# Fifty-two steps in seven products instead of twenty-two, with the scan's work cut into pieces between them

## The chip, the core and the metric

The kernel runs on one core of a Trainium2 chip. A core has TensorE (matrix products, PE in the profile, its weight loads PEld), VectorE (DVE), ScalarE (ACT), GpSimd (POOL) and SyncE (SP, which here only issues DMAs). Each engine takes its own instructions strictly in the order in which the kernel issues them, and waits on semaphores for data of the others. TensorE writes into PSUM, eight banks of 128 x 512 float32. The metric is the device time of one execution in microseconds (us).

## The reference

Two blocks follow each other. The first is a state-space scan over 4 sequences of 8 heads and 768 positions, in chunks; the second is a feed-forward layer over all 3072 tokens with the gate h * cos(h):

```python
M = CB * L                                   # L = exp(cum_i - cum_j), causal
y_intra = np.einsum('bhij,bhjd->bhid', M, xc)
y_inter = np.einsum('bhin,bhnd->bhid', Cc, state) * decay_to_i[..., None]
state = decay_full * state + np.sum(Bx, axis=2)
...
h = x @ w_in          # x: the scan's y, 3072 x 256;  w_in: 256 x 2048
g = h * np.cos(h)
out = g @ w_out       # w_out: 2048 x 256
```

All of it is in float32.

## The kernel before, in words

The 768 positions are NC = 6 chunks of 128, each of two units of 64. The feed-forward part is a loop of NC * NF = 96 steps n; with NF = 16, c = n // 16 is the chunk and f = n mod 16. In chunks after the first, steps f = 0 to 7 belong to the first unit (u = 0) and 8 to 15 to the second; a step works on 256 columns of h, turned (hp, 128 x 512, one PSUM bank), for one unit of all four sequences.

One step is a chain over the engines: TensorE makes hp (`first`, L660), ScalarE rounds hp / 2 pi to an integer k (`wind_k`, L667), VectorE subtracts it (`wind_w`, tile w, L673), ScalarE takes the sine (`gate`, L682), VectorE multiplies by hp (`gated`, tile gT, L687), and TensorE multiplies by w_out into o (`second`), LAG = 3 steps later. PSUM holds two banks for hp (tag "h"), two for o, and two pairs of banks (tag "scan") that the scan uses.

From chunk 1 on, o is made by a Strassen-like scheme with seven products (`seven`, L831); GpSimd makes the differences of gT (`differ`, L712 to L715). At the end of a unit `end7` copies o's two banks on ScalarE (L849, L852), and the copies are summed into the output (`rest`, L864) on VectorE or GpSimd; `finished` holds the second copy back to the start of the next step where that one is in `sevens`.

In 22 of the 96 steps hp too is made by seven products (`begin7`, `period7`, L760): steps 42 to 44, 58 to 60, 74 to 76 and 81 to 93. A step of seven issues on TensorE: products 1, 5 and 7 of its hp; two products of o; the last pair (3 and 4) of the previous step's hp; the next two products of o; the late pair (6 and 2); three more of o. Between the first three and the late pair, ScalarE copies what the first three left (L764, L765); after the late pair VectorE adds the copies (L768, L770) before the last pair may come. Its k, w, sine and gT run a step later. A third hp bank is taken from a pair where three such steps follow each other. The scheme needs differences of y (`differ_y`, tile m, L742) and of w_in (`differ_in`, L731).

The scan of chunk e = c + 1 runs beside the steps of chunk c, at places set by the table `steps`: decays (`decays0`, a scan on VectorE, L375, of 128 x 512), the reach (`reaches`, L574: eight scans of 64 elements), transposes of the blocks of B and C (`turn_blocks`, L582), masked copies of C on ScalarE and a product with the reach (`turn2`, L591 and L593), the products g of C and B (`inner2`, L603), their weighing on VectorE (`weights`, L465), the state (`add_state`, four operations, L498), the products with the state (`open2`, L617, and the sums of the new state, L477), the rest of y (`finish2`, L629), and its copies (L636, L489). `open2` stands at f = 13, `finish2` at f = 15.

All loads go through SyncE's queue in the order of issue: the `blocks` of a chunk (L147, L150), `along` (the decays spread over partitions, L188), `arow` (L165), B, C and x, and the outputs.

Of the kernel before, what the change touches and what calls it, by code (L numbers as in the profile page):

```python
# [25 lines left out]
def kernel(  # L26
# [51 lines left out]
    ones = const.tile([P, P], FP32, name="ones")  # L78
    V.memset(ones, 1.0)
# [98 lines left out]
    def load_along(c, seqs=range(NB)):  # L178

        if c >= NC:  # L180
            return
        if c not in along:
            along[c] = rows.tile([P, NB, P], FP32, tag="along", bufs=2, name="along")
        for b in seqs:
            s = b // 2
            for q in range(4 if s else 1):
                rs, hs = (group(q, s), slice(2 * q, 2 * q + 2)) if s else (slice(0, P), slice(0, H))
                nc.sync.dma_start(  # L188
                    out=along[c][rs, b], in_=a_all[b, hs, c * P:(c + 1) * P].unsqueeze(1)
                    .to_broadcast([hs.stop - hs.start, N, P]))  # L190
# [7 lines left out]
    lead, along1, reach1 = (ms[2][:, i * NB * (W + 1):(i + 1) * NB * (W + 1)]  # L198
                            .rearrange("p (b i) -> p b i", b=NB) for i in range(3))
# [155 lines left out]
    reach, part, yT, after = {}, {}, {}, {}  # L355
# [12 lines left out]
    def decays0(k, p, i=0, n=1):  # L368
# [5 lines left out]
        rows_ = spread.pop((k, p, i)) if k < 2 else arows[k][:, p]  # L374
# [118 lines left out]
    def add_state(k):  # L493

        for s in range(2):
            for p in range(2):
                i = k % 2 * W + W - 1
                V.scalar_tensor_tensor(out=after[k][:, s, p], in0=after[k - 1][:, s, p],  # L498
                                       scalar=reach[k // 2, s][:, p, i:i + 1],
                                       in1=after[k][:, s, p], op0=ALU.mult, op1=ALU.add)  # L500
# [66 lines left out]
    def reaches(c, b):  # L567

        s, p = divmod(b, 2)
        if p == 0:  # L570
            reach[c, s] = scan.tile([P, 2, P], FP32, tag="reach", name="reach")
        for k in range(2):
            i = slice(k * W, (k + 1) * W)
            V.tensor_tensor_scan(out=reach[c, s][:, p, i], data0=along[c][:, b, i],  # L574
                                 data1=ones[:, 0:W], initial=1.0, op0=ALU.mult, op1=ALU.mult)
# [3 lines left out]
    def turn_blocks(c, s):  # L579
        turned[c, s] = t = scan.tile([P, 2, 2, P], FP32, tag="turned", bufs=2, name="turned")  # L580
        for k in range(2):
            V.transpose(out=t[:, k].rearrange("p s (t m) -> p s m t", m=4),  # L582
                        in_=blocks[c, s][:, k].rearrange("p h s (m n) -> p (s m) h n", m=4))
        del blocks[c, s]

    def turn2(c, s):

        tp = turned.pop((c, s))
        cT = scan.tile([P, 2, 2, P], FP32, tag="cT2", bufs=2, name="cT2")
        for t in range(2):  # L590
            ACT.activation(cT[:, :, t], tp[:, 1], AF.Copy, scale=slot[:, t:t + 1])  # L591
        rT = scan.tile([P, 2, P], FP32, tag="rT", name="rT")
        V.tensor_tensor(out=rT, in0=tp[:, 1], in1=reach[c, s], op=ALU.mult)  # L593
        part[c, s] = (tp[:, 0], cT, rT)

    def inner2(c):

        g = [pair("g") for _ in range(2)]
        for k, p, s, q in ((k, p, s, q) for k in range(2) for p in range(2) for s in range(2)
                           for q in range(4)):  # L600
            bT, cT, _ = part[c, s]
# [9 lines left out]
    def open2(c):  # L611

        ys[c] = y = [pair("y") for _ in range(2)]
        for k, p, s, q in ((k, p, s, q) for k in range(2) for p in range(2) for s in range(2)
# [3 lines left out]
                      rhs=part[c, s][2][r, p, k * W:(k + 1) * W], start=(k == p == 0), stop=False,  # L618
# [350 lines left out]
    def rest_of_loads():  # L969
# [21 lines left out]
        for k in (4, 5):  # L991
            for s in range(2):
# [4 lines left out]
    steps = {c: dict(reach=(5, 6), turn=(6, 7), inner=8, weigh=(9, 10), state=(-NF, 12),  # L997
                     decays=(8, 11, 13, 14), along=(12, 13)) if c == 2 else
             dict(reach=(1, 2), turn=(3, 4), inner=5, weigh=(6, 7), state=(0, 5),
                  decays=(8, 9, 14, 15), along=(6, 7)) for c in range(2, NC)}  # L1000
# [12 lines left out]
    def decays2(k, p):  # L1013
        decays0(k, p)
        if p == 1:
# [7 lines left out]
    AHEAD = 4  # L1023
# [3 lines left out]
    runs = [*(range(NF * c + 10, NF * c + 13) for c in range(2, NC - 1)),  # L1027
            range(NC * NF - 15, NC * NF - 2)]
    sevens = {n: r for r in runs for n in r}
    at_ = {}  # L1030

    def bank_of(n):

        i = n - sevens.get(n, sevens.get(n - 1))[0]
        if i == 0:
            at_["hp"] = pair("hp")[:, 0]
        return at_["hp"] if i % 3 == 1 else bank([P, TB], "hp", "h")
# [6 lines left out]
    def period7(n):  # L1044
# [17 lines left out]
        return last_  # L1062
# [55 lines left out]
    for n in range(AHEAD, NC * NF + LAG):  # L1118
        c, f = divmod(n, NF)
        if n < NC * NF:  # L1120

            if c > 0 and f in (loads_of := (6, 7, 8, 9) if c == 1 else (0, 1, 2, 3)):
                load(c + 2, loads_of.index(f))
# [10 lines left out]
            second_ = lambda n=n: second(n - LAG)  # L1134
            if n in sevens:
                second_ = period7(n)
            elif n - 1 in sevens:
                first(n, rest7[n - 1][2], to_=bank_of(n))
                gates(n - 1)
            else:  # L1140
                first(n)
            closing = f == NF - 1 and 1 <= c < NC - 1
            take_y = finish2(c + 1) if closing else None
            if n not in sevens:
                wind_k(n)
                wind_w(n)
# [8 lines left out]
            if n not in sevens:  # L1155
                gate(n)
# [5 lines left out]
            if joins:  # L1162
# [4 lines left out]
            behind += [lambda c=c, b=2 * s + p: reaches(c, b) for c, s in chunks_at(n, "reach")  # L1167
                       for p in range(2)]
# [100 lines left out]
```

## Time and profile before

| | |
|---|---|
| three runs | 366.31, 367.38, 367.40 us; median 367.38 |
| profiled execution | 366.6 us, span 364.7 us, granted clock of TensorE 0.999 |
| TensorE | 356.8 us busy, 98% of the span |
| VectorE, ScalarE, GpSimd | 259.0, 191.6, 234.1 us busy |
| hp plain (L660) | 592 matmuls of 128x256, 141.7 us |
| hp in seven (L760) | 308 matmuls of 128x128 |
| DMA | 26.42 MB, 72 GB/s on average |

A float32 product shows as two matmul records. The records of matmuls overlap, so the distance between starts, not the mean length of a record, is what a product costs. In the lines of a timeline the columns are start, duration, engine, line, operation, output and inputs, shapes, count of merged instructions, and in brackets the idle time before and what ended it.

### The profile page before, as it was taken

The numbers are of one execution on the slowest core, as the hardware profiler recorded it, in microseconds if no ns is written. First come the engines' busy times: TensorE is split into PE (matmuls) and PEld (weight loads), VectorE is DVE, ScalarE is ACT, GpSimd is POOL, SyncE is SP. The second block draws the span as 40 slices with busy tenths as digits, with TensorE's granted clock in tenths as the row PEclk, the third lists the DMA queues.
The fourth block names the chain that finished last, engine by engine and source line by source line (L and its number), as shares of the span: only waits on it lengthen the run. The fifth ranks groups of instructions, "written<-read, shape, count | busy, mean of one in ns | idle before, by whom it ended". The sixth has DMA issues, their size and how long they took to land.

```text
span 364.7 us, 10134 instructions
## 1 busy us (share of the span) xinstructions
PE 356.8 (98%) x4034; PEld 326.0 (89%) x4034; DVE 259.0 (71%) x448; ACT 191.6 (53%) x368; POOL 234.1 (64%) x375
## 2 busy tenths in 40 slices
PE   8997999999999999999999999999999999999995
PEld 5686888888999999999999999989999999999995
DVE  7789998587867867976665887556786455566663
ACT  4597766445445254635554544545553644566651
POOL 6567757579856873467587467487656384375572
PEclk9999999999999999999999999999999999999999
DMA  7996956691665528214007621001010001001002
GB/s 140 260 373 137 224 132 81 112 119 51 128 102 75 92 60 129 44 44 86 8 4 111 74 71 34 3 3 40 0 31 0 2 2 31 2 3 31 2 0 59
DMA packets 97327, 26.42 MB, mean 72 GB/s; under 512 B 87328, under 2 KB 93184, under 8 KB 97280
## 3 DMA queue, kind: packets, MB, share of 16 engines
q1 hardware_dynamic: 96032, 25.38, 34.7%
q8 instruction: 32, 0.52, 0.6%
q10 hardware_dynamic: 1248, 0.39, 0.5%
q14 instruction: 15, 0.12, 0.1%
HBM read 22.36 MB, written 3.34 MB: 70 GB/s over the span
## 4 chain that ended last, share of the span: by engine, by line
PE 95%; DVE 2%; ACT 1%; issue 1%; ACTq 0%; DVEq 0%
PE hp L660 35%; PE o L831 34%; PE hp L760 9%; PE o L790 7%; PE y L629 2%; PE g L603 1%; PE y L477 1%; PE y L617 1%; PE g L456 1%; PE a_ps L364 1%; PE warm L84 1%; PE y L525 1%; PE y L515 1%; PE o L891 0%; DVE mag L261 0%
## 5 line engine op out<-in xcount | busy, mean ns | idle before, releaser
L660 PE MATMUL hp<-yT,w_in 128*128 128x256 f32 x592 | 141.7, 382 | 2.1 <-DVE gT L687 2.1
L660 PEld LDWEIGHTS hp<-yT,w_in 128*128 128x128 f32 x592 | 107.5, 190 | 16.4 <-POOL mag L249 2.5
L673 DVE SCALAR_TENSOR_TENSOR w<-hp,k 128x512 f32<-128x512 f32 x96 | 66.1, 688 | 68.6 <-ACT k L667 68.4
L712 POOL TENSOR_TENSOR gd<-gT 128x256 f32<-128x256 f32 x79 | 60.0, 760 | 82.6 <-DVE gT L687 67.7
L682 ACT ACTIVATE w<-w,quarter 128x512 f32<-128x512 f32 x96 | 69.4, 723 | 66.3 <-DVE w L673 66.0
L667 ACT ACTIVATE k<-hp 128x512 int32<-128x512 f32 x96 | 57.2, 596 | 74.7 <-PE hp L660 68.0
L687 DVE TENSOR_TENSOR gT<-hp,w 128x512 f32<-128x512 f32 x96 | 65.6, 684 | 23.3 <-ACT w L682 17.7
L831 PE MATMUL o<-words,gd 128*128 128x128 f32 x474 | 69.4, 275 | 0.0
L831 PEld LDWEIGHTS o<-words,gd 128*128 128x128 f32 x474 | 61.0, 192 | 0.0
L831 PE MATMUL o<-w_out,gT 128*128 128x128 f32 x316 | 49.7, 276 | 0.3 <-ACT ps L849 0.3
L831 PEld LDWEIGHTS o<-w_out,gT 128*128 128x128 f32 x316 | 46.1, 191 | 3.5 <-ACT ps L849 0.5
L715 POOL TENSOR_TENSOR gd<-gT,gd 128x128 f32<-128x128 f32 x79 | 40.8, 516 | 6.2
L714 POOL TENSOR_TENSOR gd<-gT,gd 128x128 f32<-128x128 f32 x79 | 39.3, 497 | 6.2
L831 PE MATMUL o<-w_out,gd 128*128 128x128 f32 x158 | 30.6, 275 | 0.0
L831 PE MATMUL o<-words,gT 128*128 128x128 f32 x158 | 30.5, 275 | 0.0
L790 PE MATMUL o<-w_out,gT 128*128 128x256 f32 x128 | 30.1, 379 | 0.0
L375 DVE TENSOR_TENSOR_SCAN lam<-arow,unit 128x512 f32<-128x512 f32 x20 | 29.0, 1448 | 0.0
L790 PEld LDWEIGHTS o<-w_out,gT 128*128 128x128 f32 x128 | 24.2, 190 | 3.2
L831 PEld LDWEIGHTS o<-words,gT 128*128 128x128 f32 x158 | 24.0, 192 | 0.0
L831 PEld LDWEIGHTS o<-w_out,gd 128*128 128x128 f32 x158 | 24.0, 192 | 0.0
L760 PE MATMUL hp<-m,wid 128*128 128x128 f32 x132 | 22.3, 278 | 0.0
L760 PEld LDWEIGHTS hp<-m,wid 128*128 128x128 f32 x132 | 18.2, 192 | 0.2
(129 smaller groups left out, 424.0 us busy)
## 6 DMA issues: line engine op xcount, KB each, us to landing
words<-in_moe_w_in_dram SPq DMA_DIRECT2D x8, 512.0 KB
words<-in_moe_w_out_dram SPq DMA_DIRECT2D x8, 512.0 KB
xr<-in_x_dram SPq DMA_DIRECT2D x24, 128.0 KB
arow<-a_cut SPq DMA_DIRECT2D x10, 256.0 KB
arow<-a_cut SPq DMA_DIRECT2D x10, 252.0 KB
out_dram<-sum SPq DMA_DIRECT2D x18, 128.0 KB
bc<-in_B_dram SPq DMA_DIRECT2D x24, 64.0 KB
blocks<-in_B_dram SPq DMA_DIRECT2D x16, 32.0 KB
```

The costliest lines, as they stand in the source:

```text
L375: V.tensor_tensor_scan(out=lams[k][:, p, hs].rearrange(flat), data0=rows_.rearrange(flat), data1=unit0[:, hs].rearrange(flat), initial=0.0 ...
L660: PE.matmul(to_[:, e], lhsT=w_in[:, k, fs], rhs=y[:, k], start=(k == 0), stop=(k == KT - 1), skip_group_check=True)
L667: ACT.activation(k, hp[n], AF.Copy, bias=0.25, scale=INV_2PI)
L673: V.scalar_tensor_tensor(out=w, in0=hp[n], scalar=INV_2PI, in1=k, op0=ALU.mult, op1=ALU.subtract)
L682: ACT.activation(cos, cos, AF.Sin, bias=quarter, scale=TWO_PI)
L687: V.tensor_tensor(out=gT[n], in0=hp.pop(n), in1=cos, op=ALU.mult)
L712: G.tensor_tensor(out=d[:, 0:2], in0=g[:, 1:2].to_broadcast([P, 2, P]), in1=g[:, 3::-3], op=ALU.subtract)
L714: G.tensor_tensor(out=d[:, 2], in0=g[:, 0], in1=d[:, 0], op=ALU.subtract)
L715: G.tensor_tensor(out=d[:, 3], in0=g[:, 2], in1=d[:, 2], op=ALU.subtract)
L760: PE.matmul(at[:, i], lhsT=w[q], rhs=y_[q], start=(q == 1), stop=True, skip_group_check=True)
L790: PE.matmul(o[c, u][:, t], lhsT=g[:, 2 * e + t], rhs=w_out[:, 2 * j + e], start=(j == e == t == 0), stop=(j == NJ - 1 and e == 1), skip_gr ...
L831: PE.matmul(at[q], lhsT=a_[q], rhs=w[q], start=(j == 0 and q in starts), stop=(j == NJ - 1), skip_group_check=True)
```

## The change

Steps in seven products become 52: 33 to 36, 39 to 44, 46 to 52, 55 to 60, 62 to 68, 71 to 76 and 78 to 93. From step 32 on a second main loop runs, in which the scan's work is handed to the steps as a list (`scan_work`), at most one or two small pieces each; `steps` remains for chunk 2 alone.

- The chunk's g and its weighing become one visit at f = 5 (`visit_g`), and the whole of y (`open2`, `finish2`, copies) one visit at f = 13 (`visit_y`); steps 5 and 13 make hp plainly, and so does step 6.
- The reach of two sequences becomes one scan of 260 elements; for it `along` has a leading zero for every run of 64, and its loads are split in two (20 instead of 10 DMAs a chunk). `lead` (a one ahead of 64 zeros) becomes a tile of its own, and the tile of ones goes.
- The state is advanced by two operations over all of it instead of four.
- Half of the decays are done in halves (128 x 256), in steps 7 to 10; the others in the visit of y.
- The differences of the next y for its first unit are made on GpSimd, two at f = 14 and two at f = 15; the output sums from step 32 on are all on GpSimd, one a step.
- In steps 5 to 23 o follows hp by two steps; step 5 makes o of steps 2 and 3, step 24 makes none, and from step 25 the lag is three again.
- The differences of w_in are made at other steps (`in_at`).

The diff, cut:

```diff
-    ones = const.tile([P, P], FP32, name="ones")
-    V.memset(ones, 1.0)
+    lead = const.tile([P, NB, W + 1], FP32, name="lead")
...
-            along[c] = rows.tile([P, NB, P], FP32, tag="along", bufs=2, name="along")
+            along[c] = rows.tile([P, NB, 2, W + 1], FP32, tag="along", bufs=2, name="along")
+            G.memset(along[c][:, :, :, 0:1], 0.0)
...
-                nc.sync.dma_start(
-                    out=along[c][rs, b], in_=a_all[b, hs, c * P:(c + 1) * P].unsqueeze(1)
-                    .to_broadcast([hs.stop - hs.start, N, P]))
+                for k in range(2):
+                    nc.sync.dma_start(
+                        out=along[c][rs, b, k, 1:],
+                        in_=a_all[b, hs, (2 * c + k) * W:(2 * c + k + 1) * W].unsqueeze(1)
+                        .to_broadcast([hs.stop - hs.start, N, W]))
...
     def add_state(k):
-        for s in range(2):
-            for p in range(2):
-                i = k % 2 * W + W - 1
-                V.scalar_tensor_tensor(out=after[k][:, s, p], in0=after[k - 1][:, s, p],
-                                       scalar=reach[k // 2, s][:, p, i:i + 1],
-                                       in1=after[k][:, s, p], op0=ALU.mult, op1=ALU.add)
+        r = reach[k // 2][:, :, :, k % 2, W:].to_broadcast([P, 2, 2, 2 * D])
+        dec = scan.tile([P, 2, 2, 2 * D], FP32, tag="whole", bufs=1, name="whole")
+        V.tensor_tensor(out=dec, in0=after[k - 1], in1=r, op=ALU.mult)
+        V.tensor_tensor(out=after[k], in0=after[k], in1=dec, op=ALU.add)
...
+    def reaches(c, s):
+        V.tensor_tensor_scan(
+            out=reach[c][:, s].rearrange(flat), data0=along[c][:, 2 * s:2 * s + 2].rearrange(flat),
+            data1=lead.rearrange("p b i -> p (b i)"), initial=0.0, op0=ALU.mult, op1=ALU.add)
...
+    in_at = {24: slice(1, 3), 28: slice(3, 5), 32: slice(0, 1), 35: slice(7, 8), 41: slice(5, 7)}
-    runs = [*(range(NF * c + 10, NF * c + 13) for c in range(2, NC - 1)),
-            range(NC * NF - 15, NC * NF - 2)]
+    runs = [r for c in range(2, NC - 1) for r in (
+                range(NF * c + (1 if c == 2 else -2), NF * c + 5), range(NF * c + 7, NF * c + 13))]
+    runs.append(range(NF * (NC - 1) - 2, NC * NF - 2))
...
+        third = n % 3 == 1 if c == NC - 1 else f in (2, 7, 10, 15)
+        return pair("hp")[:, 0] if third else bank([P, TB], "hp", "h")
...
-    def period7(n):
+    def period7(n, extra=()):
...
-        return last_
+        for do in extra:
+            do()
+        last_()
...
+        if n == AHEAD + 1:
             second(n - LAG)
-        elif n > AHEAD:
-            second_()
+        if n > AHEAD and n != LATER:
+            second(n - (LAG if n > LATER else LAG - 1))
...
+    def visit_g(n, e):
+        inner2(e)
+        rest7[n - 1][2]()
+        wind_k(n - 1)
+        second(n - LAG)
+        weights(2 * e, 0)
+        wind_w(n - 1)
+        weights(2 * e, 1)
+        gate(n - 1)
+        gated(n - 1)
+        first(n)
+        for q in range(2):
+            weights(2 * e + 1, q)
+        gates(n)
+    def visit_y(n, e, halves):
+        open2(e)
+        rest7[n - 1][2]()
+        wind_k(n - 1)
+        take_y = finish2(e)
+        second(n - LAG)
+        first(n)
+        for do in halves[:1]:
+            do()
+        wind_w(n - 1)
+        gate(n - 1)
+        for do in halves[1:]:
+            do()
+        gated(n - 1)
+        for k in range(2):
+            take_y(k)
+        gates(n)
...
+    def scan_work(c, f):
+        e, k = c + 1, 2 * c + 4
+        work = {15: [lambda: mask_c(e + 1, 0, 0)], 14: [lambda: add_state(2 * e + 1)],
+                0: [lambda: reaches(e, 0)],
+                1: [lambda: turn_blocks(e, 1, (1,))],
+                2: [lambda: turn_blocks(e, 1, (0,)), lambda: mask_c(e, 1, 0)],
+                3: [lambda: reaches(e, 1), lambda: mask_c(e, 1, 1)],
+                4: [lambda: reach_c(e, 0)],
+                6: [lambda: reach_c(e, 1), lambda: add_state(2 * e)],
+                11: [lambda: turn_blocks(e + 1, 0, (1,))],
+                12: [lambda: turn_blocks(e + 1, 0, (0,))]}
+        work[0].append(lambda: mask_c(e, 0, 1))
...
+        for i in range(4 if e < NC - 1 else 0):
+            work[7 + i] = [lambda i=i: half_decay(k, i // 2, i % 2)]
...
+        if live and f in (14, 15):
+            for i in range(2 * (f - 14), 2 * (f - 14) + 2):
+                differ_y(e, i, G, slice(0, 1))
```

For c = 2 the list differs: the transposes of the first half of chunk 3 come at step 32, and the reach of chunk 3 at steps 35 and 36.

## The prediction

> Times are in us. A step is one n of the main loop, f = n mod 16 its place in a chunk, T the start of its first hp product on TensorE.
>
> **What bounds the kernel now.** I read the busy shares first, then the chain that ended last, then TensorE's timeline, the other engines' timeline in a run of seven-product steps, and SyncE's queue.
>
> ```profile
> span 364.7 us, 10134 instructions
> PE 356.8 (98%) x4034; PEld 326.0 (89%) x4034; DVE 259.0 (71%) x448; ACT 191.6 (53%) x368; POOL 234.1 (64%) x375
> PE 95%; DVE 2%; ACT 1%; issue 1%; ACTq 0%; DVEq 0%
> ```
>
> TensorE is never idle for long: its work is the time. So a saving counts in full only if TensorE goes on without waiting, and every wait that is added counts in full too. The timeline gives the length of both kinds of step:
>
> ```profile
> 197.72 1.89 PE L660 MATMUL hp<-yT,w_in 128*128 128x256 f32 x8
> 201.01 1.89 PE L660 MATMUL hp<-yT,w_in 128*128 128x256 f32 x8
> ...
> 326.86 0.39 PE L760 MATMUL hp<-yT,w_in 128*128 128x128 f32 x2
> 328.87 0.39 PE L760 MATMUL hp<-m,wid 128*128 128x128 f32 x2
> 329.99 0.39 PE L760 MATMUL hp<-yT,w_in 128*128 128x128 f32 x2
> ```
>
> A plain step takes 201.01 - 197.72 = 3.29, a step of seven 329.99 - 326.86 = 3.13. The line at 328.87 is the "late pair" of the seven (products 6 and 2): it is due at T + 2.01, and at T + 1.56 where the step before was plain and left no last pair. It must wait for the two ACT copies of its step. What runs around it:
>
> ```profile
> 326.13 0.69 DVE L673 SCALAR_TENSOR_TENSOR w<-hp,k 128x512 f32<-128x512 f32 x1 [0.88 <-ACT k L667]
> 326.74 0.42 DVE L768 TENSOR_TENSOR hp<-hp,m 128x256 f32<-128x256 f32 x1
> 326.86 0.72 ACT L682 ACTIVATE w<-w,quarter 128x512 f32<-128x512 f32 x1 [0.76 <-DVE w L673]
> 327.19 0.30 DVE L770 TENSOR_TENSOR hp<-hp,m 128x128 f32<-128x128 f32 x1
> 327.68 0.69 DVE L687 TENSOR_TENSOR gT<-hp,w 128x512 f32<-128x512 f32 x1 [0.19 <-ACT w L682]
> 327.73 0.37 ACT L764 COPY m<-hp 128x256 f32<-128x256 f32 x1 [0.16 <-PE hp L760]
> 328.14 0.25 ACT L765 COPY hp<-hp 128x128 f32<-128x128 f32 x1
> 328.51 0.73 POOL L712 TENSOR_TENSOR gd<-gT 128x256 f32<-128x256 f32 x1 [0.64 <-DVE gT L687]
> 328.63 0.60 ACT L667 ACTIVATE k<-hp 128x512 int32<-128x512 f32 x1 [0.24 <-PE hp L760]
> 329.32 0.46 POOL L714 TENSOR_TENSOR gd<-gT,gd 128x128 f32<-128x128 f32 x1
> 329.86 0.46 POOL L715 TENSOR_TENSOR gd<-gT,gd 128x128 f32<-128x128 f32 x1
> ```
>
> With T = 326.86: the sine of the step before ends at T + 0.72, the copies run from T + 0.87 to T + 1.53, k starts at T + 1.77, gT of the step before ends at T + 1.51, POOL's differences of it end at T + 3.46. VectorE is free from T + 1.51 to T + 2.40 (next w): a piece of up to 0.9 fits there. ACT has only 0.15 between sine and copies.
>
> **What the change takes away.** 30 more steps of seven at 3.29 - 3.13 = 0.16 each: 4.7. The starts of the three old middle runs had about 0.1 each: 0.3. This is all of the gain. The pieces on VectorE (half decays, two half transposes, one reach scan; nearest rows 0.62 to 0.75 for half of a 1.21 to 1.45 scan, 0.64, 1.12 for the 128x260 scan) lie in the 0.9 gap; 1.12 overshoots by 0.26, and the sums have 0.4 before the last pair waits for them. I cost them at nothing; without that slack see the third rival. VectorE gains 30 x 0.72 of sums and loses 12 output sums (8.0 + 1.8, now on POOL) and some state work, about 12 net on 259: not a bound over the whole. POOL has room over a chunk too (about 45 of 57), but its order matters below. The removed fill of ones and the moved memsets lie in the first us or beside other work: nothing.
>
> **The lag.** Step 5 now takes o of two steps. In the trace hp of step 6 starts at 34.35 after 2.08 idle, set by gT of step 4, so the extra 1.73 fits into that idle time. The same o is then missing at step 24. There TensorE comes at 104.51 to inner2, which needs the C masks that ACT finishes at 105.34 + 0.91 = 106.25; it started at 106.16 before. So the missing o is only an earlier wait: gain 0, at most 1.6 if the masks came early. In steps 5 to 23 the shorter lag leaves w_out's pieces and gd in time by the rows (closest: step 20, 0.2 late): 0.2, left out.
>
> **SyncE's queue.** load_along goes from 10 issues a chunk to 20. What stands behind them in the queue:
>
> ```profile
> 82.95 5.08 SPq L188 DMA_DIRECT2D along<-a_all  x8
> 99.41 2.19 SPq L150 DMA_DIRECT2D blocks<-in_C_dram  x2
> ...
> 104.64 0.66 DVE L582 STREAM_TRANSPOSE turned<-blocks 128x256 f32<-128x256 f32 x1 [0.96 <-DMA blocks<-in_C_dram]
> ```
>
> SyncE issues back to back from 52 to 145. Eight issues take 5.08, 0.635 each (median 0.583 for 16 KB and for 64 KB alike), so ten more take 6.35 even at half the bytes. About 1.5 of small waits (ob, arow) between 88 and 99 absorb part: the C blocks of chunk 2 come 4.85 later, and their transpose waits for them already today. gT of step 23 and inner2 stand behind it: **+4.85** (bounds 1.6, at half the issue time, and 6.35). The along loads of chunk 3 push the C blocks of chunk 3 again by 6.35, less 0.5: issued to 138.25 + 10.6, plus 3.0 landing (101.60 to 104.64) makes 151.9. Their transpose now stands in step 33, VectorE at 137.33 + 4.85 + 2.9 = 145.1. w, the sums and the sine of 33, and the output copy of step 34 follow; o of step 35, due at 148.8, starts at 154.95: **+6.1**, with the copy of the next paragraph in it (bounds 1.1 and 8).
>
> **Output copies.** Twice a chunk o leaves its banks inside a run of seven, after steps f=2 and f=10. Step 83 of the trace shows the price: the copy starts at 314.41, behind the sine, o waits until 314.92, and the step takes 317.48 - 313.79 = 3.69, that is 0.56 more. At f=10 this is new three times: 1.7. At f=2 a mask (0.45) now stands ahead of the copy on ACT: 1.1 each in chunks 3 and 4: 2.2.
>
> **Visit of y (f=13).** hp of step 13 is the last thing before step 14's seven. k (T + 0.26 to 0.86), w, sine end at T + 2.4, then come the copies on ACT, to T + 3.1; the late pair is due at T + 1.56. Before, a whole o (1.56) lay between. Stall 1.57, and 1.84 where four state scalings (1.18) stand ahead of k: 1.84 + 1.84 + 1.57 = **5.25**.
>
> **Difference of y.** POOL's last two differences of the next y are issued at f=15 behind gd of step 14, which ends at T + 3.46 of step 0; the third (0.46) ends at T + 3.99; the late pair of step 0, due at T + 2.01, reads it. Stall 1.95, at steps 48, 64, 80: **5.85**.
>
> **Visit of g (f=5).** VectorE gets four weights (4 x 0.68) among w and gT of steps 4 to 6, reach_c 0.42 and add_state about 1. By these rows gT of step 4 ends at the moment hp of step 6 wants its bank (0.3), the sine of step 6 ends 1.8 after step 7 began, and step 7's late pair waits 1.0: 1.3 x 3 = **3.9**, the least sure term (0 to 6).
>
> Sum: -4.7 - 0.3 + 4.85 + 6.1 + 1.7 + 2.2 + 5.25 + 5.85 + 3.9 = +24.9. The profiled execution took 366.6 (span 364.7 and 1.9 around it), 0.8 under the median of the three runs, 367.38. 366.6 + 24.9 = **391.5**.
>
> **A rule weighed.** The two DMA waits leave TensorE idle for some 6 each; the longest idle stretch of the trace after the start is 2.08, and the granted clock stayed at full in it, so no row prices a longer one and the sum has 0. The Trainium skill, "TensorE: Matmul & The Clock Gate", section "What's actually happening", says that an idle window of about 3.4 halves the clock until about 3.4 of busy time have passed. By that page an estimate of up to 1.7 comes on top at each gap, and the sum would be 395.
>
> **Rivals.** (1) Faster: the steps of seven follow each other as in the last run of the trace, 13 steps at 3.13 with one stall, and every new wait finds its data. That gives 366.6 - 5.0 = 361.6. For it: the 0.9 gap on VectorE. Against it: the waits after f=13 and f=15 follow from single engines' order and durations. It decides where all stalls together stay under 4.7; the two alone are 11.1. (2) The queue is hidden: SyncE's issues get cheaper with their bytes, or the blocks are there in time. Then 11 of the sum goes, but the f=2 copy of chunk 2 (1.1) is back: 366.6 + 24.9 - 9.85 = 381.7. Against it stands the 0.96 that VectorE waits today. (3) VectorE is the bound: w, sums and gT take 2.1 plus gaps of 0.25, a contended piece 1.0; then ten steps a chunk overrun by about 0.2 each, 6 in all: 397.5. (4) The waits are there but half of them overlap: 366.6 - 5 + 15 = 376.6.
>
> **How the numbers follow.** Forecast 0.56 (386 to 397), hidden queue 0.20 (377 to 386), VectorE 0.07, half of the waits 0.08, faster 0.07, no change 0.02 (within 0.3%, what a measurement of this kernel can tell). The range 372 to 398 leaves out the last two, some of the fourth case and of the third: under 0.2. Slower 0.91.
>
> **What would show it.** TensorE's idle time grows from about 8 to over 30. In the waits: hp late pairs on ACT's copy at steps 7 and 14 of a chunk, on POOL's difference at step 0, o on the output copy; VectorE on the blocks' DMA at steps 23 and 33; L188's count at 80. The forecast is wrong if the late pairs don't wait, or if SyncE's queue has caught up by step 23.

## The result, and the profile after

The changed kernel takes 399.94 us (median of four executions, 398.41 to 401.46) against 367.31 for the kernel before (four executions, 366.31 to 367.40): a ratio of 1.0895, 95% interval [1.0847, 1.0943]. Ratios here and below go by the executions within 1.5% of the fastest of the same kernel, which leaves out four of the ten of c4_split_visit (370.63 to 372.92) and one of the kernel before beside it. The prediction was 391.5 with a range of 372 to 398; slower was right, the size was not. The profiled execution took 398.41, 31.8 more than that of before.

The head of the page and the chain that ended last, after:

```profile
span 396.6 us, 10628 instructions
PE 360.0 (91%) x4214; PEld 330.7 (83%) x4214; DVE 266.6 (67%) x457; ACT 208.3 (53%) x428; POOL 254.1 (64%) x419
PE 54%; SPq 15%; POOL 8%; ACT 7%; DVE 7%; issue 4%; DMA 4%; DVEq 0%; POOLq 0%; ACTq 0%
```

TensorE's share of the chain fell from 95% to 54%. What came in is SyncE's queue (15%) and, in small parts, every other engine. TensorE's busy time rose by 3.2, though it has less to do; that is a first sign of a slower clock in places. What TensorE waits for, after (total, times, longest):

```profile
PE hp L768 <- POOL m L750: 5.7, 4, 1.7
PE g L611 <- ACT cT L589: 5.7, 2, 5.0
PE o L839 <- ACT ps L857: 4.4, 7, 1.8
PE hp L768 <- DVE hp L778: 3.8, 2, 3.0
PE hp L768 <- ACT hp L773: 3.6, 3, 1.2
PE hp L668 <- DVE gT L695: 2.5, 3, 1.5
PE hp L768 <- POOL along L183: 1.8, 1, 1.8
PE hp L668 <- issue: 1.2, 1, 1.2
PE y L637 <- issue: 1.0, 1, 1.0
```

No single wait is the loss: nine kinds of 1 to 6 each. Busy records of matmuls overlap, so I made a ledger from starts: the distance from one matmul's start to the next, less the median distance that this kind of matmul (its tiles and shape) has in the kernel before. The sum of the medians is TensorE's work, the excess its gaps; the absolute sums depend by some us on how kinds are told apart, the differences between kernels less. Before: work 336.8, gaps 17.8. After: work 332.0, gaps 55.0. So the steps of seven saved 4.8 (6.4 where each kernel's own medians by line, tiles and shape are used), and the gaps took 37.2. Where the gaps are, by the prediction's steps:

| step of the prediction | predicted | measured (excess of the waiting matmul) |
|---|---|---|
| work saved, old run starts | -4.7, -0.3 | -4.8 |
| the lag, and SyncE's queue at step 24 | 0 + 4.85 | 5.29 at step 24, less 1.73 at step 6 (2.24 to 0.51): 3.56 |
| the queue at step 35, with the copy there | 6.1 | 1.99 |
| output copies, f=10 and f=2 | 1.7, 2.2 | 1.39, 1.72 |
| visit of y, late pair of step 14 | 5.25 | 3 x 1.37 = 4.11 |
| difference of y, steps 48, 64, 80 | 5.85 | 3 x 1.90 = 5.70 |
| visit of g, steps 55, 56, 71 and 72 | 3.9 | 0.23 + 0.64 + 0.23 + 0.25 = 1.35 |
| **not in the prediction:** last pair behind a transpose, steps 44 and 60 | - | 1.05 + 3.18 |
| half clock after the gaps of steps 24 and 60 | 0 in the sum (1.7 each as an estimate by the page) | about 1.7 each |
| differences of w_in late, steps 39 and 40 | - | 1.94 + 0.81 |
| "issue" waits in the visits of y | - | 1.37 + 1.16 |
| hp of steps 94 and 95 waits for its bank | - | 1.66 + 0.79 |
| masks at step 37 | - | 0.88 |

The list's 1.8 behind `POOL along L183` is the wait of step 39: the fill of the leading zeros, 0.11 long, stands right behind a difference of w_in on GpSimd, and a1 below, which has no such fill, keeps the same 1.94 behind that difference. The predicted waits of 29.9 came to 19.8. The others, not predicted, are 16.2, and some 1.1 is in pieces under 0.3.

Step 24 in the timeline of after (start, duration, engine, line, operation, output and inputs; in brackets the idle time and what ended it):

```profile
104.32 0.64 DVE L582 STREAM_TRANSPOSE turned<-blocks 128x256 f32<-128x256 f32 x1 [1.37 <-DMA blocks<-in_B_dram]
104.42 0.45 PE L611 MATMUL g<-cT,turned 32*64 32x128 f32 x8
108.27 0.63 DVE L582 STREAM_TRANSPOSE turned<-blocks 128x256 f32<-128x256 f32 x1 [3.31 <-DMA blocks<-in_C_dram]
108.93 0.91 ACT L589 ACTIVATE cT<-turned,slot 128x256 f32<-128x256 f32 x2 [3.75 <-DVE turned L582]
109.89 1.99 PE L611 MATMUL g<-cT,turned 32*64 32x128 f32 x56 [5.03 <-ACT cT L589]
```

The transpose of C, at 104.64 before, comes at 108.27; the masks follow, and TensorE stands from 104.9 to 109.89. The table by windows shows what comes on top (window, length, busy time of PE, PEld, DVE, ACT, POOL, then the granted clock):

```profile
110.00:113.40 3.40, 3.40 (x60) 2.80 (x61) 2.55 (x4) 0.72 (x1) 3.24 (x6) 0.51 0.76 116
113.40:116.80 3.40, 3.40 (x25) 3.17 (x24) 1.29 (x2) 1.32 (x2) 3.17 (x7) 1.00 0.62 103
256.70:260.10 3.40, 3.40 (x134) 3.00 (x135) 3.40 (x5) 0.73 (x2) 2.40 (x4) 0.50 0.13 29
```

After each of the two longest gaps (5.3 and 3.2) TensorE runs at half its clock for 3.4, which is about 1.7 of work lost (an estimate, 3.4 x 0.5).

The second of these gaps was in no step of the prediction. Its origin is in SyncE's queue, after:

```profile
234.63 1.35 SPq L875 DMA_DIRECT2D out_dram<-sum  x2
236.03 1.21 SPq L146 DMA_DIRECT2D blocks<-in_C_dram  x2
237.28 2.84 SPq L189 DMA_DIRECT2D along<-a_all  x4
240.16 1.15 SPq L146 DMA_DIRECT2D blocks<-in_B_dram  x2
241.36 10.08 SPq L189 DMA_DIRECT2D along<-a_all  x16
251.48 1.20 SPq L146 DMA_DIRECT2D blocks<-in_C_dram  x2
```

```profile
254.69 0.63 DVE L582 STREAM_TRANSPOSE turned<-blocks 128x256 f32<-128x256 f32 x1 [4.62 <-DMA blocks<-in_C_dram]
255.18 0.67 DVE L681 SCALAR_TENSOR_TENSOR w<-hp,k 128x512 f32<-128x512 f32 x1
256.22 0.30 DVE L778 TENSOR_TENSOR hp<-hp,m 128x128 f32<-128x128 f32 x1
256.58 0.74 PE L768 MATMUL hp<-yT,wid 128*128 128x128 f32 x2 [2.98 <-DVE hp L778]
```

The queue stands for 18.4, to 234.63, behind an output whose sum POOL makes one piece a step; then come the 20 loads of `along`, and only then the blocks that VectorE transposes at f=11. VectorE waits 4.62 for them, with w and the sums of the next step behind, and the last pair waits for the sums.

The two predicted waits that came out best, in the timeline of after. First the late pair of step 14, then that of step 48:

```profile
197.78 0.60 ACT L675 ACTIVATE k<-hp 128x512 int32<-128x512 f32 x1 [0.83 <-PE hp L668]
199.13 0.72 ACT L690 ACTIVATE w<-w,quarter 128x512 f32<-128x512 f32 x1 [0.76 <-DVE w L681]
199.76 0.35 ACT L772 COPY m<-hp 128x256 f32<-128x256 f32 x1
200.14 0.25 ACT L773 COPY hp<-hp 128x128 f32<-128x128 f32 x1
200.45 0.49 PE L768 MATMUL hp<-m,wid 128*128 128x128 f32 x2 [1.21 <-ACT hp L773]
...
208.19 0.99 POOL L750 TENSOR_TENSOR m<-yT,m 128x128 f32<-128x128 f32 x2
208.70 0.49 PE L768 MATMUL hp<-m,wid 128*128 128x128 f32 x2 [1.74 <-POOL m L750]
```

k, w and sine of the plain step 13 stand ahead of the two copies; and POOL's third difference (the first of the two merged at 208.19) is what the pair of step 48 reads.

### The profile page after: what moved, and what is told of

Read it like the earlier page. It is cut to its first block, busy times and chain, and to the rows that moved or that the text cites. A ratio compares the mean times of both kernels' runs of the same rounds, so it can differ in the third digit from the quotient of the medians.

```text
span 396.6 us, 10628 instructions
## 1 busy us (share of the span) xinstructions
PE 360.0 (91%) x4214; PEld 330.7 (83%) x4214; DVE 266.6 (67%) x457; ACT 208.3 (53%) x428; POOL 254.1 (64%) x419
## 4 chain that ended last, share of the span: by engine, by line
PE 54%; SPq 15%; POOL 8%; ACT 7%; DVE 7%; issue 4%; DMA 4%; DVEq 0%; POOLq 0%; ACTq 0%
PE o L839 17%; PE hp L668 13%; PE hp L768 12%; SPq L189 9%; PE o L798 5%; DVE w L681 3%; DMA blocks<-in_C_dram 3%; ACT w L690 3%; POOL gd L720 2%; ACT k L675 2%; SPq L149 2%; POOL gd L722 2%; SPq L146 1%; DVE gT L695 1%; POOL gd L723 1%
## 5 line engine op out<-in xcount | busy, mean ns | idle before, releaser
L720 POOL TENSOR_TENSOR gd<-gT 128x256 f32<-128x256 f32 x79 | 63.2, 800 | 94.0 <-DVE gT L695 86.4
L668 PE MATMUL hp<-yT,w_in 128*128 128x256 f32 x352 | 84.2, 385 | 3.7 <-DVE gT L695 2.5
L668 PEld LDWEIGHTS hp<-yT,w_in 128*128 128x128 f32 x352 | 64.9, 192 | 13.8 <-issue 3.6
L839 PE MATMUL o<-words,gd 128*128 128x128 f32 x474 | 74.4, 275 | 0.2 <-POOL gd L722 0.2
L768 PE MATMUL hp<-m,wid 128*128 128x128 f32 x312 | 53.0, 279 | 11.3 <-POOL m L750 5.7
L768 PEld LDWEIGHTS hp<-m,wid 128*128 128x128 f32 x312 | 43.1, 192 | 13.5 <-POOL m L750 6.7
L839 PEld LDWEIGHTS o<-w_out,gT 128*128 128x128 f32 x316 | 43.6, 192 | 7.1 <-ACT ps L857 5.7
L768 PE MATMUL hp<-yT,w_in 128*128 128x128 f32 x208 | 40.2, 275 | 0.0
L772 ACT COPY m<-hp 128x256 f32<-128x256 f32 x52 | 19.1, 368 | 25.2 <-PE hp L768 25.1
L768 PEld LDWEIGHTS hp<-yT,w_in 128*128 128x128 f32 x208 | 31.8, 192 | 0.2
L798 PE MATMUL o<-w_out,gT 128*128 128x256 f32 x128 | 29.9, 379 | 0.0
L377 DVE TENSOR_TENSOR_SCAN lam<-arow,unit 128x512 f32<-128x512 f32 (+1 forms) x24 | 29.7, 1240 | 0.0
```

Source lines behind the costliest of these rows:

```text
L668: PE.matmul(to_[:, e], lhsT=w_in[:, k, fs], rhs=y[:, k], start=(k == 0), stop=(k == KT - 1), skip_group_check=True)
L720: G.tensor_tensor(out=d[:, 0:2], in0=g[:, 1:2].to_broadcast([P, 2, P]), in1=g[:, 3::-3], op=ALU.subtract)
L768: PE.matmul(at[:, i], lhsT=w[q], rhs=y_[q], start=(q == 1), stop=True, skip_group_check=True)
L798: PE.matmul(o[c, u][:, t], lhsT=g[:, 2 * e + t], rhs=w_out[:, 2 * j + e], start=(j == e == t == 0), stop=(j == NJ - 1 and e == 1), skip_gr ...
L839: PE.matmul(at[q], lhsT=a_[q], rhs=w[q], start=(j == 0 and q in starts), stop=(j == NJ - 1), skip_group_check=True)
```

## Experiments

All kernels compute the whole output. Ratios are to the kernel before, run beside them on the same chip; the changed kernel's is 1.0895. The kernel before took 367.31 beside the changed kernel and 367.9 to 368.1 beside the others, so a difference of medians to the 399.94 of the changed kernel is uncertain by up to 0.8; the ratios don't have this error.

**The loads of `along`, undone (a1_along_one).** In the changed kernel the leading zero is stored in DRAM, so that a sequence loads in one DMA again (rows of 130 elements):

```diff
-    a_all = dram.tile([NB, H, S], FP32, name="a_all")
+    a_all = dram.tile([NB, H, 2 * NC, W + 1], FP32, name="a_all")
...
-            G.memset(along[c][:, :, :, 0:1], 0.0)
...
-                for k in range(2):
-                    nc.sync.dma_start(
-                        out=along[c][rs, b, k, 1:],
-                        in_=a_all[b, hs, (2 * c + k) * W:(2 * c + k + 1) * W].unsqueeze(1)
-                        .to_broadcast([hs.stop - hs.start, N, W]))
+                nc.sync.dma_start(
+                    out=along[c][rs, b].rearrange("p k i -> p (k i)"),
+                    in_=a_all[b, hs, 2 * c:2 * c + 2].rearrange("h k i -> h (k i)").unsqueeze(1)
+                    .to_broadcast([hs.stop - hs.start, N, 2 * (W + 1)]))
...
```

> The changed kernel, with the loads of along in 10 DMAs a chunk again (the leading zeros are stored in a_all, so that a row of 130 comes in one piece); nothing else is changed. Theory (SyncE's queue sets the waits on the blocks): the waits of VectorE on the C blocks at steps 23, 33, 43 and 59 go (12.8 us in all in the profile), with them TensorE's 5.3 at step 24, 1.1 of the 2.0 at step 35, 1.05 at step 44 and 3.2 at step 60, and the two stretches of half clock (1.7 each): about 14 less, near 386. Rival (the transposes at f = 11 wait because they stand earlier than before, whatever the number of DMAs): only step 24 and 35 gain, about 8 less, near 392.

Measured: 389.67 (387.79 to 389.89), ratio 1.0594 [1.0561, 1.0626], 10.3 less (11.1 by the ratios). In its profile the gap of step 24 is 1.42, that of step 35 is 0.86, and those of steps 44 and 60 are gone.

```profile
PE g L609 <- ACT cT L587: 1.8, 2, 1.2
```

VectorE's waits for blocks of C, 12.8 in the changed kernel, came down to 0.3. The theory's 14 is not reached, and by its time alone the kernel lies between theory and rival. Its profile says why: 1.42 stays at step 24, where TensorE waits for ScalarE's masks, and a new stretch of half clock at 325.84 takes about 1.7 back. The rival's premise, that the gaps at f=11 stay, is refuted: they are the queue's too. The queue is the largest single cause, about a third of the 32.6.

**The same loads alone, in the kernel before (b1_split_along).** The opposite test: nothing but the split, same bytes.

```diff
+                for k in range(2):
                     nc.sync.dma_start(
-                    out=along[c][rs, b], in_=a_all[b, hs, c * P:(c + 1) * P].unsqueeze(1)
-                    .to_broadcast([hs.stop - hs.start, N, P]))
+                        out=along[c][rs, b, k * W:(k + 1) * W],
+                        in_=a_all[b, hs, (2 * c + k) * W:(2 * c + k + 1) * W].unsqueeze(1)
+                        .to_broadcast([hs.stop - hs.start, N, W]))
```

> The kernel before, with nothing changed but that each load of along is split into two halves of 64 (20 DMAs a chunk instead of 10, the same bytes). Theory (the issue time on SyncE counts, 0.6 a DMA): the C blocks of chunk 2 come some 4 to 6 late, VectorE waits for them at step 23, and TensorE with it: 4 to 7 more, near 373, the most of it before step 26; later chunks have slack in that kernel. Rival (the issue time follows the bytes, or other work hides it): 0 to 2 more.

Measured: 374.8 (371.85 to 376.73), ratio 1.0191 [1.0127, 1.0255]: 6.9 lost, with an interval of 4.7 to 9.4. What VectorE waits for, in this kernel, and what TensorE waits for:

```profile
DVE turned L584 <- DMA blocks<-in_C_dram: 5.1, 1, 5.1
```

```profile
PE g L605 <- ACT cT L593: 4.8, 1, 4.8
```

The bytes are the same and the chain from blocks over transpose and masks to `inner2` is the one above. The issue of the C blocks ends 5.0 later than in the kernel before (106.61 instead of 101.60), and their transpose starts 6.4 later (111.01 instead of 104.64). So the number of issues on SyncE is most of the cost; 1.4 is a longer way from issue to transpose, the cause of which is open (the loads' share of the DMA engines is 34.5%, and 34.7% before). As in the changed kernel, half clock follows the gap (3.41 from 113.06, about 1.7).

**hp before o in the visit of y (a2_hp_before_o).**

```diff
         take_y = finish2(e)
-        second(n - LAG)
         first(n)
+        second(n - LAG)
```

> The changed kernel, with hp of step 13 ahead of o in the visit of y; nothing else is changed. Theory (the late pair of step 14 waits because k, w, sine and copies follow hp too closely): the 1.37 at steps 46, 62 and 78 go, 4.1 less, near 396. Rival (VectorE or ScalarE is the limit there, and another wait takes its place at once): under 1 less.

Measured: 396.19 (395.02 to 397.19), ratio 1.0781 [1.075, 1.0812]: 3.75 less. The 1.37 is gone at steps 62 and 78; 0.85 of it stays at 46. So the late pair waits because nothing lies between hp of step 13 and step 14, as the prediction had it.

**All four differences of y at f=14 (a3_dy_early).**

```diff
-        if live and f in (14, 15):
-            for i in range(2 * (f - 14), 2 * (f - 14) + 2):
+        if live and f == 14:
+            for i in range(4):
                 differ_y(e, i, G, slice(0, 1))
```

> The changed kernel, with all four differences of the next y at f = 14, ahead of the differences of gT of step 14 on GpSimd; nothing else is changed. Theory (the order on GpSimd makes the late pair of steps 48, 64 and 80 wait): the three waits of 1.9 go, 5.7 less, near 394. Rival (GpSimd is full there, and the differences of gT come late for o instead): under 2 less, with new waits of o on gd.

Measured: 392.79 (391.66 to 396.5), ratio 1.0707 [1.0648, 1.0767]: 7.15 less. The three waits of 1.90 are gone (5.7); the rest is within the spread of the executions.

**The lag of three throughout (a4_lag3).**

```diff
-        if n == AHEAD + 1:
-            second(n - LAG)
-        if n > AHEAD and n != LATER:
-            second(n - (LAG if n > LATER else LAG - 1))
+        if n > AHEAD:
+            second(n - LAG)
```

> The changed kernel, with o three steps behind hp throughout (step 5 makes o of step 2 alone, step 24 makes one again). Theory (the earlier o only moves a wait: 1.73 of idle time at step 6 comes back, and inner2 of step 24 waits 1.6 less): within 1 of the changed kernel, 399 to 401. Rival (the earlier o is a gain): 1.7 more, near 401.6.

Measured: 401.94 (398.23 to 403.42), ratio 1.0904 [1.0846, 1.0962]. The median lies where the rival put it, the ratio 0.3 above the changed kernel's; with executions 5 apart, theory and rival can't be told apart. In the profile the gap of step 6 is back at 2.23, and that of step 24 is 4.90, where an o more ahead of it should have left about 3.6. It is not shorter because the queue too comes later: SyncE's own waits between 88 and 106 (for w, rT, gd and others) are 3.1 instead of 0.9, and the C blocks are issued at 106.30 instead of 103.41. Half clock follows the gap of step 6 here (3.41 from 34.89). The prediction's 0 for the lag is consistent with the times, not more.

**The bank of the last plain step (a5_last_bank).** Before, hp of step 94 was in a bank of the pair; after, it takes one of the two "h" banks, which gT of step 92 reads last.

```diff
-            first(n, rest7[n - 1][2] if n - 1 in sevens else None)
+            first(n, rest7[n - 1][2] if n - 1 in sevens else None,
+                  to_=pair("hp")[:, 0] if n == NC * NF - 2 else None)
```

The place in the timeline of after: TensorE starts when gT ends (0.69 from 378.96, and the way to TensorE).

```profile
378.96 0.69 DVE L695 TENSOR_TENSOR gT<-hp,w 128x512 f32<-128x512 f32 x1 [0.19 <-ACT w L690]
379.80 1.10 PE L668 MATMUL hp<-yT,w_in 128*128 128x256 f32 x4 [1.49 <-DVE gT L695]
```

> The changed kernel, with hp of step 94 in a bank of the pairs, as in the kernel before, instead of one of the two hp banks. Theory (the waits of hp on gT at steps 94 and 95, 1.66 and 0.79 in the profile, come from the bank alone, a point that the prediction left out): 1.7 to 2.4 less, near 397.8. Rival (the chain over ScalarE and VectorE sets the end whatever the bank): under 0.5 less.

Measured: 399.02 (398.76 to 400.28), ratio 1.0847 [1.0822, 1.0872]: 0.9 less by the medians, 1.8 by the ratios, whose intervals overlap, so that the theory's 1.7 to 2.4 is neither shown nor refuted by the time. The waits at 94 and 95 are gone from its profile (2.45). The profiled execution is the longest of the four (400.28): it has half clock for 17.1 against 6.8 in the changed kernel's, and an "issue" wait of 2.73 stands at 197.62, in the visit of y, where the changed kernel has 1.37. This made the "issue" waits the next question.

**All mends together (c1_all), and o after the last pair (c2_late_o).** c1 has a1, a2, a3 and a5, and three moves for the smaller gaps: a step's second extra piece goes behind its last three products of o (so the mask no longer stands ahead of the output copy), the differences of w_in at 32 and 35 go to 31 and 34 with their slices exchanged, and those of y's second unit start at f=3. c2 adds, for the steps at which o begins in a new pair of banks, the last pair ahead of o's first two products:

```diff
+        swap = n - 1 in sevens and (n - LAG) % NJ == 0
+        if not swap:
             first_()
         if n - 1 in sevens:
             rest7[n - 1][2]()
             wind_k(n - 1)
+        if swap:
+            first_()
         then()
```

> The changed kernel with all of the single mends together: along in 10 DMAs, hp ahead of o in the visit of y, the differences of y at f = 14 and (second unit) f = 3 to 6, the last bank, the second of two pieces of a step behind the copy of o, the differences of w_in for j = 7 and 0 at steps 31 and 34. Theory (the waits add): 10.3 + 3.7 + 7.1 as measured alone, 2.2 for the bank, 1.2 for the mask, 2.7 for w_in and 1.2 for the second unit are 28 less: near 371.5. Rival (engines are full, and waits take each other's place): above 380.

> The one with all mends, and in the steps where o begins new banks (f = 3 and 11) the last pair of the previous hp goes ahead of the first two products of o, so that the copy of the old o has 0.45 more time. Theory (the seven waits of o on that copy, 0.46 each, are a matter of order): 2.5 to 3.2 less than with all mends. Rival (the last pair waits for VectorE's sums instead): under 1 less.

Measured: c1 373.42 (372.6 to 374.4), ratio 1.0153 [1.0127, 1.0179]; c2 370.41 (370.12 to 375.1), ratio 1.0097 [1.0046, 1.0147]. By the ledger c1's gaps are 29.3, c2's 26.5, at work 332.0 in both. The seven waits of 0.46 behind output copies, at f=3 and f=11, are gone in c2; at f=3 the late pair waits 0.18 instead, three times. That is the theory's 3 by the medians, though the intervals of c1 and c2 overlap. The parts add up, nearly: c1 was to be 28 less and is 26.5 less, and what the ledger named, when mended, brought back 26.5 (c1) and 29.5 (c2) of the 32.6. In c2 the largest waits left are:

```profile
PE y L635 <- issue: 3.0, 3, 1.5
PE g L609 <- ACT cT L587: 1.8, 2, 1.2
PE o L837 <- issue: 0.9, 1, 0.9
```

**The masks of C earlier (c3_masks_up).**

```diff
+            for e, s in chunks_at(n - 1, "turn")[:n == NF + 8]:
+                turn2(e, s)
             wind_k(n)
...
-            work[3] = [lambda: reaches(e, 0), lambda: mask_c(e, 1, 0)]
-            work[4] = [lambda: reaches(e, 1), lambda: mask_c(e, 1, 1)]
+            work[3] = [lambda: reaches(e, 0), lambda: mask_c(e, 1, 0), lambda: mask_c(e, 1, 1)]
+            work[4] = [lambda: reaches(e, 1)]
```

> The kernel of c2_late_o, with two edits to the masked copies of C on ScalarE: in step 24 they are issued ahead of k (they waited for k there, though their transposes were done about 1.1 us earlier), and for chunk 3 both masks of the second half go to step 35 (one was in step 36, after its last products). The trace of c2_late_o shows TensorE waiting 1.16 at 106.27 (the group before inner2 included, 1.40) and about 0.9 at step 37 for these masks. Theory (TensorE waits for ScalarE's order there, not for the DMA any more): both go, k of step 24 moves by 0.3 and has slack; 370.4 - 1.1 - 0.9 = about 368.4. Rival (the next wait in line, gT or the weighing, takes their place): 369.5 to 370.5.

Measured: 370.81 (369.61 to 371.84), ratio 1.0100 [1.0075, 1.0124]: no gain over c2; the theory missed. The mask waits did shrink (1.42 to 0.95 at step 24, 0.90 to none at step 37). But the "issue" waits of this profile are 2.23, 1.98, 1.29 and 0.93, 6.4 against 4.7 in c2. In these two profiles they took the place of what was saved.

**The visit of y pulled apart (c4_split_visit).** Between the products with the state and the rest of y now lie hp and a whole o; the scalings of the state go to step 14.

```diff
         open2(e)
         rest7[n - 1][2]()
         wind_k(n - 1)
-        take_y = finish2(e)
         first(n)
         second(n - LAG)
...
         gated(n - 1)
-        for k in range(2):
-            take_y(k)
+        take_y = finish2(e)
         gates(n)
+        for k in range(2):
+            take_y(k)
```

> c3_masks_up with the visit of y reordered: products with the state and sums of the new state (128 small products in a row), then the last pair, hp of step 13 and a whole o, and only then the rest of y (128 more); the four scalings of the state go from ahead of k to step 14. Theory: the waits that the trace lists as issue at the visits of y are TensorE's instruction stream running dry. The trace of c2_late_o has 33 fetches of 16 KB of instructions in all; one lands at 181.39, and the rest of y resumes at 182.81; the next lands at 186.41, and o resumes at 187.78: each time 1.4 later. Small products use up a fetch in about 3 us, larger ones in some 12. Spread out, the waits (1.63 and 0.93 in the first visit, 0.9 to 1.0 in the two others, 4.5 together) mostly go, and step 14's late pair waits up to 0.4 three times: 368.4 - 4.5 + 0.8 = about 364.5, under the kernel before. Rival 1 (the number of small products in the visit sets the waits, wherever they stand): no gain, 368 to 369. Rival 2 (ScalarE's order in the visit gives the gain back at step 14): 366 to 368.

Measured: 370.29 (365.10 to 372.92, ten executions), ratio 1.0014 [0.9963, 1.0064]. By the ratios this is 0.9% under c3 and level with the kernel before, by the medians of all executions 0.5 under c3's 370.81. The executions spread by 7.8, so a gain over c3 is not firm, and the theory's 364.5 is not reached. The profiled execution took 370.63, with half clock for 6.83 from 186.61. In the second and third visit the "issue" waits (1.29 and 0.93 in c3) are gone. In the first there is now one of 3.0:

```profile
PE y L635 <- issue: 3.0, 1, 3.0
```

So in two of three visits, here and in c5's profile below, the place matters and not the number of small products (against rival 1), and the late pair of step 14 waits at most 0.21 (against rival 2). What is left is the first visit.

**One load moved out of the first visit (c5_arow_later).** Only there two loads of `arow` are under way. The load for unit 11 goes from the visit (step 45) to step 48:

```diff
-            if k + 2 < 2 * NC:
+            if k + 2 < 2 * NC - 1:
                 load_arow(k + 2)
...
+            if n == 3 * NF:
+                load_arow(2 * NC - 1)
```

> c4_split_visit with one load moved: arow of unit 11 (two DMAs of 252 KB in rows of 252 bytes) is issued at step 48 instead of in the visit of y of step 45. In c4_split_visit the waits called issue are gone from the second and third visit of y (1.29 and 0.93 before), while the first has one of 3.18 at 187.46: the fetch of instructions before it starts only at 184.98, 5.6 after the one before, and between 181.5 and 185 the 16 DMA engines are filled by arow's rows. Theory (the fetch stands behind the load in the DMA engines): the wait of the first visit goes, 2.5 to 3.2 less; undisturbed executions of c4_split_visit at 365 to 370 become 364 to 367. Rival (where a block of instructions ends decides, not the load): the wait stays at about 3 and the time does not move.

Measured: 366.68 (365.79 to 370.55, nine executions) against 368.09, ratio 0.9962 [0.9947, 0.9977]: faster than the kernel before by 0.4%. Part of this may be the clock: eight of the nine have a mean clock of 0.999 or 1.000, of the thirteen of the kernel before beside them only five have 0.998 or more, and against these five (median 367.42) the eight (median 366.5) are 0.9 faster. The profiled execution is the longest of the nine (370.55), in which step 24 waits 2.7 for the masks; even so its "issue" wait in the visit is 1.1 instead of 3.0:

```profile
PE g L609 <- ACT cT L587: 2.7, 1, 2.7
PE y L635 <- issue: 1.1, 1, 1.1
```

The busy share of the DMA engines from 174 to 190, in 40 slices, first in c4, then in c5:

```profile
DMA  4211017679969921000077799374000000000100
```

```profile
DMA  0100100112221110087799898210000000200000
```

In c4 there are two bursts of `arow`, and the second runs to 184.8, right where TensorE runs dry (184.5); in c5, whose visit comes 4.3 later, there is one. This speaks for the theory, and the rival's wait of about 3 is not there. But the intervals of c4 and c5 overlap a little, the two kernels ran on different chips, and one profile each, both of executions above the median, is not much, so that the load delays the fetch is likely and not shown.

## Why the prediction was wrong, and where it was right

**Work saved, -4.7.** Right: 4.8 by the ledger, and it is also all that the change gives.

**The lag, 0.** Consistent: step 6 gave 1.73, step 24 lost an o that would have covered as much; a4 could not tell a difference. What the term left out is the clock: the gap of step 6, which the earlier o closes, is followed by half clock in the profiles of a4 and b1.

**SyncE's queue.** The mechanism was right, and a1 and b1 show it from both sides. The sizes were off: 4.85 was 3.56 at step 24 (inside its bounds), and 6.1 was 1.99 at step 35. The second failed at "issued to 138.25 + 10.6": it carried both delays on to chunk 3's blocks, whose issue ended at 145.3. The sum gave 148.85 there, 3.6 too late: SyncE's small waits between the two loads of `along` took up more of the second delay than the 0.5 that I allowed.

**Pieces on VectorE, "I cost them at nothing".** This is the step that failed most: a term of 0 that measured 4.2, and 5.9 with the half clock after it. I compared the duration of each piece with the 0.9 gap and did not ask what its data wait for. The transposes at f=11 moved ahead as well, to a place behind 20 issues of `along`; VectorE waited there for the C blocks, and TensorE for VectorE's sums: 1.05 at step 44 and 3.18 at step 60, gone in a1. I had followed the queue for chunks 2 and 3 and stopped there. (The 1.12 of the reach scan overshoots the 0.9 by 0.22, not by 0.26; no wait here hangs on it.)

**Output copies, late pair, difference of y.** Right in place and cause: 1.7 was 1.39 and 2.2 was 1.72; 5.25 was 4.11, since the four scalings ahead of k cost nothing on top (1.37 in all three visits); 5.85 was 5.70. a2 and a3 give these back.

**Visit of g.** 3.9 was 1.35, inside its 0 to 6, but the mechanism holds only for a third of it: the late pairs of steps 55 and 71 wait 0.23 each for ScalarE, not 1.0. The other 0.89 is two late pairs a step later, which wait for POOL's difference of y's second unit; and the one that waits longest, in step 39, waits for POOL's differences of w_in.

**"A rule weighed".** The sum had 0 for the clock. The rule of the Trainium skill, "TensorE: Matmul & The Clock Gate", section "What's actually happening", would have been nearer: the two gaps of 5.3 and 3.2 are each followed by 3.41 at a clock of 0.5. The trace agrees on the length of the stretch and not on the condition, for the second gap is shorter than the window of 3.4 that the rule asks for. My argument against it was that no row of the trace showed a longer gap. That is a reason to be unsure, and not one for zero.

**What no step spoke of.** The bank of step 94 (2.45) was in the diff, in the rule for the third bank; the differences of w_in (2.75) are in the list of changes, and the prediction never placed them on POOL; of the "issue" waits (2.5) the profile of before has one alone, of 0.34 at 15.88.

Of the rivals, (1), (2) and (4) fell with the waits that are there; (3) gave nearly the same time by another cause, and VectorE, at 67%, did not bind. So that the total of 24.9 came as near the measured 32.4 (37.2 less 4.8) as it did is partly luck: terms too large by 10 stood against missing ones of 16.

## What to carry to other kernels

When work is cut up and moved, follow the data of every moved piece back to its DMA and through the queue in which that is issued, for all repetitions of the loop and not only the first. Price a queue by its number of issues: here twice as many loads of half the size cost 6.9, more than the 4.8 of work that the change saved. Where one engine is busy for 98% of the time, every wait that a reordering adds counts in full: here a saving of 4.8 showed, as 0.4%, only when nearly all the added waits had been mended.

## What the hardware showed that I had not expected

**TensorE can run out of instructions.** The profile of after lists a queue of instruction loads (packets, MB, share):

```profile
q8 instruction: 33, 0.54, 0.6%
```

33 loads of 16 KB against 8536 records of TensorE (products and weight loads) make about 259 for each. The trace gives the time of every load: in the changed kernel one ends at 194.34, and the "issue" wait ends at 195.79; one ends at 319.40, and the wait at 320.76. In c2 these pairs are 181.38 and 182.81, 186.41 and 187.78; in a5 196.03 and 197.62; in c4 186.27 and 187.46. In the thirteen profiles TensorE has 28 "issue" waits over 0.3, and each ends 1.2 to 1.6 after a load has ended. The Trainium skill, "Runtime: NRT & Kernel Launch", section "Instruction fetch mechanics", says that instructions come in blocks of 16 KiB, 256 at a time, and that this is mostly hidden. The block size agrees with the count. Hidden it is not, where 256 matmul records on 32 or 64 rows follow each other: single waits of up to 3.0 in a visit, and pulling them apart removes two of three. These waits differ from profile to profile, so that an edit elsewhere seems to cost or gain a microsecond or two, as in a5 and c3.

**Half clock after shorter gaps too.** In a1 a stretch of 3.41 at 0.5 begins 0.3 after a gap of 2.18; in b1 and a4 one follows the gap of step 6 (2.25 and 2.23), which the kernel before has too (2.24) and whose profile shows it without one. So gaps of about 2 slow the clock in some executions and not in others. The stretch is 3.41 in some profiles and twice that, 6.83, in others: at the gap of step 24 in a2, a3, a4 and a5, at that of step 60 in a2 and a5, at the "issue" wait in c4. The four executions of the changed kernel have mean clocks of 0.991, 0.987, 0.983 and 0.979 and spans of 396.6, 397.6, 398.6 and 399.7. One more stretch of 3.4 at half clock lowers the mean by about 0.004 (3.4 x 0.5 of 397, an estimate), which fits the steps of the clock; that the spans grow by 1.0 a step and not by 1.7 is not explained, for only the first was profiled.

**An issue costs the same for fewer bytes.** 16 issues of `along` of 8 KB took 10.08 at 241.36, 0.63 each; 8 of 16 KB took 5.08 in the kernel before, also 0.63 each.
